# A gated mix of segmented attention and a GLU: the first segment of x comes in transposed, and two weights change queues

## The chip, the cores and the metric

The kernel runs on one core of one Trainium2 chip. The core has TensorE (PE), VectorE (DVE), ScalarE (ACT), GpSimd (POOL) and SyncE (SP); transfers are issued by SP and ACT and carried by 16 DMA engines. The metric is the device time of one execution in microseconds (us), lower is better.

## The reference

The input x has 2048 tokens of 512 features. Two branches read it, and a gate for each token mixes them:

```python
q, k, v = x @ wq, x @ wk, x @ wv              # 32 heads of 16, 4 segments of 512 tokens
for s in range(4):                             # A: attention with a memory
    a_dot = softmax(q_s @ k_s.T / 4, causal) @ v_s
    a_mem = (phi(q_s) @ M) / (phi(q_s) @ z + 1e-6)
    o_s = sigmoid(beta) * a_mem + (1 - sigmoid(beta)) * a_dot
    M, z = M + phi(k_s).T @ v_s, z + phi(k_s).sum()
a = o @ wo
b = (gelu(x @ w_gate) * (x @ w_up)) @ w_down   # B: GLU, 512 -> 1792 -> 512
g = sigmoid((x * gate_w).sum(-1))
out = g * a + (1 - g) * b
```

`phi(t)` is `t + 1` for positive t and `exp(t)` otherwise. All tensors are bf16.

## The kernel before

The kernel makes one pass over four segments of 512 tokens, `s = 0..3`. Everything that multiplies x needs it with features on the partitions: the tile `xT[s % 3]` holds four blocks `kb` of 128 features by 512 tokens. From it `project` computes for four blocks `t` of 128 columns the keys `K{s}_{t}` and queries `Q{s}_{t}` (each 4 matmuls of 512 columns into one PSUM bank, then an eviction `Kev`, `Qev`), and the values `V{s}_{m}a` and `V{s}_{m}b` for four blocks of 128 tokens. The keys are copied twice with masks into `kD` (`kpada`, `kpadb`). `glu_gate` and `glu_up` compute 14 blocks each of the GLU (`G`, `U`), `outputs` the products with `w_down` (`out`) and `wo` (`wo`), the mix (`oev`) and the store (`dma`).

Attention works in fills. A fill `st{s}_{t}{A..E}` writes scores of four head groups into all four banks of `XALL` (psX), one exponential `exp` on ACT takes all 2048 columns out, POOL masks the diagonal blocks (`msk`), and after eight key blocks `pv{s}_{t}` multiplies by the values. As there is one `XALL`, a fill waits for the exponential before it. For the memory, `phk` is computed on DVE and ACT, turned by transposing transfers (`ktr`), and multiplied with the values (`mz`); reading it takes `phq`, `nd`, `ndp` and transposing transfers of the result (`otr`).

Nothing is scheduled at run time. All work is named tasks; the string `ORDER` lists them, and each engine gets its own tasks in the order of that list. `name:d` or `name:a` says whether DVE or ACT does an eviction, `name:3` gives a PSUM bank. Waits are derived from what a task reads and writes. An engine and a DMA queue work strictly in that order, so a task that waits holds back all that follows on its engine.

The start is what the change touches. The first segment's x comes in with tokens on the partitions, in three plain transfers `x0_0` (128 KB, SP), `x0_1` (128 KB, ACT) and `x0_2` (256 KB, SP) into the tile `pt[5]`, used later for probabilities. `xtr0_{h}{p}` turns it on TensorE with an identity matrix into `XALL`, four turns each for half `h` of the tokens and pair `p` of feature blocks, and `xev0_{h}{p}` copies the turned blocks to `xT[0]`. The first keys are summed in three parts: `K0_{t}a` (blocks 2 and 3, first 256 tokens), `K0_{t}b` (blocks 0 and 1, the same tokens), `K0_{t}c` (all blocks, last 256 tokens). The key weights come as two halves, `wk1` (blocks 2 and 3) on SP and `wk0` on ACT. SP then issues `wq0` after `wk1` has landed, the gate row `gw`, `wq1` after `wk0`, `wv` after `x0_2`, `beta`, the four transposing transfers of segment 1 (`x1_0` to `x1_3`, after `wq0`), and the GLU weights in halves `wg0`, `wu1`, `wg1`, `wu0`. Six matmuls on zeros (`warm1`) run on TensorE while the first data come. Segments 1 to 3 always came by transposing transfers (line 344).

The list of early waits, as the code has it, with the names of the loads waited for at the end:

```python
ld_w("wq0", SP, wq[:, halves[0], :], wsrc(A_wq)[:, halves[0], :], [("wq", 0)], 0.25, ["wk1"])
ld_w("wq1", SP, wq[:, halves[1], :], wsrc(A_wq)[:, halves[1], :], [("wq", 1)], 0.25, ["wk0"])
ld_w("wv", SP, wv[:, :, 0:512], wsrc(A_wv), [("wv",)], 0.5, ["x0_2"])
ld_xt(1, "wq0")
```

Of the kernel before, what the change touches and what calls it, by code (L numbers as in the profile page):

```python
# [246 lines left out]
def _build(es, nc, A_x, A_wq, A_wk, A_wv, A_wo, A_beta, B_w_gate, B_w_up, B_w_down, gate_w, out):  # L247
# [216 lines left out]
    def xk(s, i):  # L464
        return [("xT", s % R_XT, i), *([("xT", 0, i, "h0")] if s == 0 else [])]

    def project(s):
        b, b3 = s % 2, s % R_XT
        k0 = [Slot() for _ in range(4)]
        for nm, kbs, h in (("a", (2, 3), 0), ("b", (0, 1), 0), ("c", (0, 1, 2, 3), 1)) if s == 0 else ():  # L470
            for t in range(4):
                one(f"K0_{t}{nm}", PE, len(kbs) * T_MM / 2, [I(lambda e, t=t, i=i, h=h: e.matmul(
                    BK[k0[t].i][:, 256 * h:256 * h + 256], wk[:, i, t * 128:(t + 1) * 128], xT[0][:, i, 256 * h:256 * h + 256],
                    start=(i == 2 - 2 * h), stop=(i == 1 + 2 * h)), [("xT", 0, i, "h0"), ("wk", i),
                    *([("xT", 0, i)] if h else [])], [bk(k0[t])]) for i in kbs], opens=(nm == "a"))
# [291 lines left out]
    XB = XALL.bitcast(BF)  # L767
    for h in range(2):
        for p in (1, 0):
            j = 2 * h + p  # L770
            one(f"xtr0_{h}{p}", PE, 4 * T_TR, [I(lambda e, q=q, kb=kb, j=j: e.transpose(
                XB[:, 1024 * j + (kb % 2) * 256 + (q % 2) * 128:1024 * j + (kb % 2) * 256 + (q % 2) * 128 + 128],
                pt[stage[0]][:, q, kb * 128:(kb + 1) * 128], ident[:, :]),
                [("xs", 0, 2 * h), ("xs", 0, 2 * h + 1), ("pt", stage[0]), ("ident",)], [("X", j)]) for kb in (2 * p, 2 * p + 1) for q in (2 * h, 2 * h + 1)])
            dst = xT[0][:, 2 * p:2 * p + 2, 256 * h:256 * h + 256]
            xin = XB[:, 1024 * j:1024 * j + 512].rearrange("p (k c) -> p k c", c=256)
            wr = [("xT", 0, kb, "h0") if h == 0 else ("xT", 0, kb) for kb in (2 * p, 2 * p + 1)]
            task(f"xev0_{h}{p}", [
                (ACT, 0.477, [I(lambda e, dst=dst, xin=xin: e.activation(dst, xin, ACTF.Copy), [("X", j)], wr)]),
                (DVE, 0.335, [I(lambda e, dst=dst, xin=xin: e.tensor_copy(dst, xin), [("X", j)], wr)])], L_DVE)  # L780

# [66 lines left out]
ld_x0_0 warm0 warm1:0 ld_x0_1 ident xtr0_01 ld_wk0 masks vones0 causal1 causal0 gwz ld_wk1 ld_x0_2 ld_wq0 xev0_01:d  # L848
ld_gw consts xtr0_00 K0_1a:1 K0_2a:2 K0_3a:3 K0_0a:0 ld_wq1 ld_wv ld_beta xtr0_10 xtr0_11 xev0_00:a K0_2b K0_3b K0_1b
K0_0b xev0_11:a xev0_10:d K0_0c Kev0_0:d kpadb0_0 kpada0_0 K0_3c Kev0_3:a K0_1c K0_2c Kev0_2:d Kev0_1:d kpada0_1  # L850
Q0_0:0 Q0_3:3 Qev0_0:a st0_0A exp0_0A ld_x1_1 ld_x1_0 ld_x1_2 ld_x1_3 gwtr:2 gwev Qev0_3:d phka0_0 Q0_1:1 V0_3b:0
V0_0b:2 V0_2a:3 Vev0_3b:d st0_0B Vev0_0b:d ld_wg0 V0_1a:0 V0_3a:2 phkb0_0 Vev0_2a:d Qev0_1:d Vev0_1a:d Vev0_3a:d
V0_2b:3 Q0_2:1 V0_0a:0 exp0_0B st0_0C exp0_0C V0_1b:2 Vev0_2b:d betab Qev0_2:d Vev0_1b:a bexp Q1_1:3 Q1_2:1 kpadb0_1
Vev0_0a:d causal msk0_0A phkc0_0 vsh0_00 vsh0_01 vsh0_20 Qev1_2:d st0_0D V1_2b:0 G0_1:2 G0_3:1 exp0_0D st0_0E
Vev1_2b:d kpada0_3 exp0_0E V1_3a:0 Vev1_3a:a kpada0_2 Gev0_1:d Gev0_3:d Qev1_1:d G0_5:2 G0_0:1 st0_1A G1_3:3 V1_1b:0
msk0_0B Gev0_5:d vsh0_21 Gev0_0:d Gev1_3:d msk0_0D gqa msk0_0C kpadb0_2 Vev1_1b:d msk0_0E pv0_0:21 exp0_1A st0_1B
gfull tp0_d00 kpadb0_3 V1_0a:3 G0_4:0 msk0_1A G1_0:2 Vev1_0a:d phka0_2 tp0_d01 Gev0_4:d exp0_1B st0_1C exp0_1C msk0_1B
msk0_1C phkb0_2 Q1_0:3 G0_2:1 V1_3b:0 gqb pvp0_00 Qev1_0:d Gev1_0:d Vev1_3b:d Gev0_2:d phkc0_2 ld_wu1 ld_wg1 ld_wu0
ktr0_1 ld_x2_0 st0_1D exp0_1D G1_2:3 K1_0:2 K1_3:0 Gev1_2:d Kev1_3:d st0_2A G0_6:1 V1_2a:3 Vev1_2a:d Gev0_6:d Kev1_0:a
gz0 msk0_1D pv0_1:20 exp0_2A st0_2B exp0_2B ktr0_2 tp0_d10 pvp0_01 tp0_d11 pvp0_10 K1_1:3 Q1_3:1 Qev1_3:d Kev1_1:d  # L860
kpadb1_3 gelu0 G0_7:2 G1_1:0 Gev1_1:d gd0_7 st0_2C G1_4:1 G0_13:3 ktr0_0 Gev1_4:d phka1_0 ld_x2_2 ld_x2_3 G0_9:0
G0_10:1 G0_12:2 gd0_9 gd0_10 gd0_13 gd0_12 G0_8:0 ld_x2_1 vsh1_21 phqa1_0 pvp0_11 vsh1_20 ld_wd1 G0_11:1 K1_2:3
kpadb1_1 ota0_0 Kev1_2:d gd0_8 gd0_11 U0_10:2 V1_0b:0 h0_10 exp0_2C U0_7:1 Q2_1:3 V1_1a:2 ktr0_3 phka1_2 kpada1_3
Vev1_0b:d h0_7 kpada1_2 Qev2_1:d Vev1_1a:a st0_2D exp0_2D U0_11:0 U0_2:1 h0_11 h0_2 phqa1_2 mz0:2 phkb1_0 mza0 phkc1_0
st0_2E U0_4:3 K2_0:0 U0_13:1 h0_4 h0_13 kpada1_0 kpadb1_0 Kev2_0:d exp0_2E st0_3A exp0_3A msk0_2A msk0_2B msk0_2C
msk0_2D msk0_2E U0_9:2 pv0_2:31 st0_3B phkb1_2 exp0_3B h0_9 tp0_d21 G1_5:0 U0_5:2 U0_8:1 Gev1_5:a gr0 phkc1_2 tp0_d20
st0_3C h0_8 K2_3:3 Kev2_3:d U0_3:0 h0_3 pvp0_21 kpada1_1 U0_6:1 h0_5 h0_6 exp0_3C phqb1_2 st0_3D Q2_0:3 Q2_3:0 U0_1:2
exp0_3D Qev2_3:a Qev2_0:d h0_1 pvp0_20 kpadb2_3 st1_0A V2_2b:1 U0_0:3 exp1_0A phqb1_0 h0_0 msk0_3A msk0_3B msk0_3C gz1
goa0 gob0 msk0_3D pv0_3:02 st1_0B exp1_0B tp0_d31 tp0_d30 K2_2:3 U0_12:2 Vev2_2b:d kpadb1_2 Kev2_2:d V2_0b:0 V2_2a:1
st1_0C Vev2_0b:a exp1_0C Vev2_2a:d kpada2_2 h0_12 kpada2_3 phqc1_2 G1_6:3 K2_1:0 Kev2_1:d V2_1b:1 msk1_0B st1_0D  # L870
exp1_0D ld_wd0 kpadb2_1 ktr1_1 vsh1_00 Gev1_6:a out0_1_0:2 out0_0_0:0 st1_0E out0_0_1 out0_1_1 V2_0a:3 exp1_0E
Vev2_1b:d mzq0 Vev2_0a:d out0_0_2 out0_1_2 msk1_0C msk1_0E msk1_0A msk1_0D goc0 G1_8:1 G1_7:3 kpada2_0 ota0_2 wev0_1:d
# [73 lines left out]
```

## Time and profile before

| what | value |
|---|---|
| median of 3 runs | 265.31 us (265.06 to 265.48) |
| the profiled execution | 265.46 us |
| its span, first to last instruction | 263.7 us |
| HBM read and written | 8.14 MB and 2.10 MB |
| x transposed, issue on SP to landing | 2.4 to 4.3 us |

The page of the profile gives for each engine its busy time, then the span in 40 slices, then the chain of work that ended last: followed back from the last instruction, at each step to what released it. A line such as `9.92 1.47 PE psD L446 x6` in that chain is a start, a length, an engine, a tile, a line of the code and a count of instructions. In the timeline the form is the same, with the operation and shapes added, and in square brackets the idle time of the engine and what ended it. SPq and ACTq are the issue of transfers by SP and ACT. In the sums by stretch the columns are the window in us, its length, the busy time and number of instructions of PE, PEld (weight loads), DVE, ACT and POOL, then the granted clock, the mean share of the DMA engines and GB/s. Some matmul records can be missing from a trace.

### The profile page before, as it was taken

The page shows a single profiled execution, that of the slowest core. Times are in us where ns is not written, and L with a number is a line of the kernel's source. Part 1 is how long each engine was busy: PE and PEld are TensorE (multiplying, and loading weights), DVE is VectorE, ACT ScalarE, POOL GpSimd, SP SyncE. Part 2 cuts the span into 40 slices and gives each one's busy share as a digit, 9 for nine tenths or more (in the row PEclk, how much of TensorE's full clock was granted, in tenths as well). Part 3 has the DMA queues.
Part 4 walks back from the last instruction along what each step waited for, and adds up shares of the span by engine and source line. Part 5 has one row for each costly group of instructions (what it writes and reads, how often), then busy time and mean ns, then how long its engine had stood idle before and what let it go on. Part 6 is the DMA issues. An engine that isn't in the chain of part 4 may idle for free.

```text
span 263.7 us, 6622 instructions
## 1 busy us (share of the span) xinstructions
PE 254.3 (96%) x2775; PEld 120.4 (46%) x2815; DVE 207.9 (79%) x427; ACT 197.7 (75%) x159; POOL 99.8 (38%) x164
## 2 busy tenths in 40 slices
...
PEclk9999999999999999999999999999999999999999
...
DMA packets 31302, 16.50 MB, mean 63 GB/s; under 512 B 20776, under 2 KB 31272, under 8 KB 31272
## 3 DMA queue, kind: packets, MB, share of 16 engines
...
HBM read 8.14 MB, written 2.10 MB: 39 GB/s over the span
## 4 chain that ended last, share of the span: by engine, by line
PE 91%; DVE 3%; DMA 3%; issue 2%; SPq 0%
PE psD L446 45%; PE psD L718 17%; PE psX L598 8%; PE psD L640 7%; PE psD L495 6%; PE psD L732 5%; DMA wq<-in_A_wq_dram 2%; DMA wk<-in_A_wk_dram 1%; PE psD L543 1%; DVE omem L557 1%; DVE ost L736 1%; DVE tT L526 0%; PE psD L573 0%; SPq L340 0%; DVE rcm L556 0%
## 5 line engine op out<-in xcount | busy, mean ns | idle before, releaser
L604 ACT ACTIVATE pt<-psX 128x2048 bf16<-128x2048 f32 x72 | 135.1, 1876 | 41.2 <-PE psX L598 41.0
L610 POOL TENSOR_TENSOR pt<-pt,ctri 128x256 bf16<-128x256 bf16 x128 | 92.2, 726 | 145.3 <-ACT pt L604 117.4
L446 PE MATMUL psD<-xT,wu 128*128 128x512 bf16 x213 | 52.4, 379 | 1.3 <-issue 0.9
L718 PE MATMUL psD<-wd,gb 128*128 128x512 bf16 x213 | 51.8, 379 | 1.2 <-issue 1.0
L446 PE MATMUL psD<-xT,wg 128*128 128x512 bf16 x214 | 51.3, 379 | 1.0 <-issue 0.5
L703 DVE TENSOR_TENSOR gb<-psD,gb 128x512 bf16<-128x512 f32 x56 | 37.4, 680 | 4.9 <-PE psD L446 4.7
L446 PEld LDWEIGHTS psD<-xT,wg 128*128 128x128 bf16 x224 | 20.7, 98 | 24.9 <-issue 1.9
L526 DVE STREAM_TRANSPOSE tT<-psD 128x512 f32<-128x512 f32 x32 | 22.3, 705 | 12.3 <-PE psD L640 12.2
L446 PEld LDWEIGHTS psD<-xT,wu 128*128 128x128 bf16 x224 | 20.6, 98 | 24.1 <-issue 1.7
L718 PEld LDWEIGHTS psD<-wd,gb 128*128 128x128 bf16 x224 | 20.3, 98 | 23.9 <-issue 2.8
L598 PE MATMUL psX<-qT,kD 32*128 32x192 bf16 (+7 forms) x512 | 28.5, 287 | 0.0
L640 PE MATMUL psD<-pt,vnat 64*17 64x128 bf16 (+7 forms) x512 | 18.7, 283 | 0.0
L651 DVE SCALAR_TENSOR_TENSOR ob<-tT,gq,rc 128x256 bf16<-128x256 f32 x32 | 17.8, 556 | 1.1
L495 PE MATMUL psD<-wv,xT 128*128 128x256 bf16 (+1 forms) x128 | 18.5, 273 | 0.0
L640 PE MATMUL psD<-pt,vsh 64*17 64x128 bf16 (+7 forms) x512 | 18.3, 283 | 0.0
L598 PEld LDWEIGHTS psX<-qT,kD 32*128 32x128 bf16 x512 | 8.2, 92 | 21.3 <-ACT pt L604 8.9
L440 DVE CAST gb<-psD 128x512 bf16<-128x512 f32 x24 | 16.0, 681 | 2.4 <-PE psD L446 2.4
L686 ACT ACTIVATE gb<-psD 128x512 bf16<-128x512 f32 x28 | 15.4, 594 | 3.1 <-PE psD L446 2.8
L736 DVE SCALAR_TENSOR_TENSOR ost<-psD,gtok,wds 128x512 bf16<-128x512 f32 (+2 forms) x18 | 12.2, 686 | 6.1 <-PE psD L732 5.3
L440 DVE CAST kT<-psD 128x512 bf16<-128x512 f32 x14 | 9.5, 687 | 8.5 <-PE psD L446 7.3
L446 PE MATMUL psD<-xT,wq 128*128 128x512 bf16 x61 | 15.5, 380 | 0.5 <-DMA wq<-in_A_wq_dram 0.2
L732 PE MATMUL psD<-wo,oT 128*128 128x512 bf16 (+2 forms) x71 | 15.8, 356 | 0.0
...
## 6 DMA issues: line engine op xcount, KB each, us to landing
...
wq<-in_A_wq_dram SPq DMA_DIRECT2D x2, 256.0 KB, 3.3
...
```

The costliest lines, as they stand in the source:

```text
L440: (DVE, 0.60, [I(lambda e: e.tensor_copy(dst, src()), [bk(sl), *reads], writes)]),
L446: one(name, PE, n * T_MM, [I(lambda e, i=i: e.matmul(BK[sl.i][:, :], lhs(i), rhs(i), start=(i == 0), stop=(i == n - 1)), reads(i), [bk(sl) ...
L495: one(f"V{s}_{m}{'ab'[hf]}", PE, 2 * T_MM, [I(lambda e, i=i, sl=sl, a=a, z=z, xs=xs: e.matmul(BK[sl.i][:, 0:z - a], xs(i), wv[:, i, a:z], ...
L526: one(f"tp{name}", DVE, 0.605, [I(lambda e, sl=sl, ti=ti: e.transpose(tT[ti][:, :], BK[sl.i][:, :]), [bk(sl)], [("tT", ti)])], bias=bias)
L598: ins.append(I(lambda e, t=t, kb=kb, ncol=ncol, c0=c0, g=g: e.matmul(XALL[:, g * 512 + c0:g * 512 + c0 + ncol], kD[b][32 * g:32 * g + 32, ...
L604: one(f"exp{s}_{name}", ACT, 2048 * 0.000833 + 0.05, [I(lambda e: e.activation(pt[slot][:, :, :], xin, ACTF.Exp, scale=ATT_SCALE), [("X",) ...
L610: ins.append(I(lambda e, mv=mv: e.tensor_tensor(mv, mv, cm, ALU.mult), [("pt", slot), ("causal",)], [("pt", slot)]))
L640: ins.append(I(lambda e, kb=kb, slot=slot, c0=c0, n=n, g=g, r0=r0, sl=banks[j], va=va: e.matmul(BK[sl.i][32 * g:32 * g + 17, 64 * kb:512], ...
L651: I(lambda e, ti=ti, ri=ri, t=t, j=j, dst=dst: e.scalar_tensor_tensor(out=dst, in0=t_rows(ti), scalar=gq[:, 2 * t + j:2 * t + j + 1], in1= ...
L703: one(f"h{s}_{ft}", DVE, 0.605, [I(lambda e, sl=sl, gi=gi, f=f: e.tensor_tensor(gb[gi][:, f, :], BK[sl.i][:, :], gb[gi][:, f, :], ALU.mult ...
L718: mm.append(I(lambda e, fb=fb, gi=gi, f=f, q=q, sl=sl: e.matmul(BK[sl.i][:, :], gb[gi][:, f, q], wd[:, fb, :], start=(fb == 0), stop=(fb = ...
L732: one(f"wo{s}_{qt}{sfx}", PE, 4 * T_MM * w / 512, [I(lambda e, kb=kb, q=q, so=so, c=c, w=w: e.matmul(BK[so.i][:, 0:w], oT[:, kb, q], wo[:, ...
```

## The change

The first segment's x is loaded like the other segments', by four transposing transfers on SP, one for each block of 128 features, blocks 3, 2, 1, 0 in this order. The turns `xtr0`, their evictions `xev0` and the plain loads of x are gone. All four early halves of `wk` and `wq` are issued by ACT: `wk1`, `wk0`, and, after `wk0` has landed, `wq1` and `wq0`. `wv` on SP waits for `x0_1`, now the transposed block 1, and segment 1's x for `wq1`. The first keys are summed one feature block at a time into `XALL` (one bank for each `t`) over all 512 tokens, and evicted from there; the first queries are two tasks each, `Q0_{t}1` (blocks 3 and 2) and `Q0_{t}0`. `ORDER` is written anew throughout; apart from these tasks it names the same ones.

```diff
-    stage = (R_PT - 1, R_PT - 2)
...
+    def ld_x0(kb):
+        load(f"x0_{kb}", SP, lambda e: e.dma_start_transpose(xT[0][:, kb, :], A_x[0, 0:512, kb * 128:(kb + 1) * 128]),
+             [("xT", 0, kb)], issue=1.31, lat=3.0)
...
-    xin0 = A_x[0, 0:512, :].rearrange("(q p) d -> p q d", p=P)
-    for eng, nm, q in ((SP, "0", slice(0, 1)), (ACT, "1", slice(1, 2))):
-        ld_w(f"x0_{nm}", eng, pt[stage[0]][:, q, :], xin0[:, q, :], [("xs", 0, q.start)], 0.125)
-    for eng, h in ((SP, 1), (ACT, 0)):
-        ld_w(f"wk{h}", eng, wk[:, halves[h], :], wsrc(A_wk)[:, halves[h], :], [("wk", 2 * h), ("wk", 2 * h + 1)], 0.25)
-    ld_w("x0_2", SP, pt[stage[0]][:, halves[1], :], xin0[:, halves[1], :], [("xs", 0, 2), ("xs", 0, 3)], 0.25)
+    for kb in (3, 2, 1, 0):
+        ld_x0(kb)
+        if kb >= 2:
+            h = kb - 2
+            ld_w(f"wk{h}", ACT, wk[:, halves[h], :], wsrc(A_wk)[:, halves[h], :], [("wk", 2 * h), ("wk", 2 * h + 1)], 0.25)
     ld_w("gw", SP, gw4, gate_w.rearrange("(kb p) -> kb p", p=P), [("gw4",), ("gwz",)], 0.01)
-    ld_w("wq0", SP, wq[:, halves[0], :], wsrc(A_wq)[:, halves[0], :], [("wq", 0)], 0.25, ["wk1"])
-    ld_w("wq1", SP, wq[:, halves[1], :], wsrc(A_wq)[:, halves[1], :], [("wq", 1)], 0.25, ["wk0"])
-    ld_w("wv", SP, wv[:, :, 0:512], wsrc(A_wv), [("wv",)], 0.5, ["x0_2"])
+    ld_w("wq1", ACT, wq[:, halves[1], :], wsrc(A_wq)[:, halves[1], :], [("wq", 1)], 0.25, ["wk0"])
+    ld_w("wq0", ACT, wq[:, halves[0], :], wsrc(A_wq)[:, halves[0], :], [("wq", 0)], 0.25, ["wk0"])
+    ld_w("wv", SP, wv[:, :, 0:512], wsrc(A_wv), [("wv",)], 0.5, ["x0_1"])
...
-    ld_xt(1, "wq0")
+    ld_xt(1, "wq1")
...
+        for kb in (3, 2, 1, 0) if s == 0 else ():
             for t in range(4):
+                one(f"K0_{t}{kb}", PE, T_MM, [I(lambda e, t=t, kb=kb: e.matmul(
+                    XALL[:, 512 * t:512 * t + 512], wk[:, kb, t * 128:(t + 1) * 128], xT[0][:, kb, :],
+                    start=(kb == 3), stop=(kb == 0)), [("xT", 0, kb), ("wk", kb)], [("X", t)])])
+        for h in (1, 0) if s == 0 else ():
+            for t in range(4):
+                one(f"Q0_{t}{h}", PE, 2 * T_MM, [I(lambda e, t=t, kb=kb: e.matmul(
+                    BK[q0[t].i][:, :], wq[:, kb, t * 128:(t + 1) * 128], xT[0][:, kb, :],
+                    start=(kb == 3), stop=(kb == 0)), [("xT", 0, kb), ("wq", h)], [bk(q0[t])])
+                    for kb in (2 * h + 1, 2 * h)], opens=(h == 1))
```

The first lines of the new order, with the start of TensorE's stream, and its last line:

```
ld_x0_3 ld_x0_2 ld_wk1 ld_x0_1 ld_x0_0 warm0 warm1:0 K0_33 K0_32 consts ld_wk0 ident gwz vones0 K0_03 K0_13 causal0
K0_02 K0_23 causal1 K0_12 masks K0_22 ld_wq1 ld_wq0 ld_gw ld_wv K0_01 K0_11 K0_31 K0_21 K0_00 K0_10 Kev0_1:a Q0_01:1
K0_30 Q0_00 K0_20 Kev0_0:d kpada0_0 kpadb0_0 Kev0_3:a Q0_31:2 gwtr:3 Q0_30 Qev0_0:a Kev0_2:d st0_0A exp0_0A kpadb0_2
gwev Q0_11:0 ld_x1_1 ld_x1_0 ld_x1_2 ld_x1_3 ld_beta V0_1b:1 Vev0_1b:d Qev0_3:d Q0_10 V0_2a:3 V0_1a:1 Qev0_1:d phka0_0
...
wo3_3c:1 wev3_3:a dma13 dma12 oev3_3c oev3_3a wo3_2:2 dma15c oev3_2 dma15a dma14 wo3_3b:3 oev3_3b dma15b
```

SP's transfers between segment 1's x and segment 2's memory read, in the new order: `beta`, `wg0`, one `vsh`, `wu1`, three `vsh`, `x2_1`, `ktr0_1`, `ktr0_0`, `wg1`, `x2_3`, `ktr0_3`, `wu0`, `x2_2`, `x2_0`, `wd1`, `ktr0_2`. Before they were: `wg0`, four `vsh`, `wu1`, `wg1`, `wu0`, `ktr0_1`, `x2_0`, `ktr0_2`, `ktr0_0`, `x2_2`, `x2_3`, `x2_1`, two `vsh`, `wd1`, `ktr0_3`. (`vsh` are copies of value rows for the second head of a pair; `ktr0` are the turns of `phk` of segment 0.)

More of the change, by code (lines that the diff above doesn't have):

```diff
@@ L464, in xk @@
     def xk(s, i):
-        return [("xT", s % R_XT, i), *([("xT", 0, i, "h0")] if s == 0 else [])]
+        return [("xT", s % R_XT, i)]
     def project(s):
         b, b3 = s % 2, s % R_XT
-        k0 = [Slot() for _ in range(4)]
-        for nm, kbs, h in (("a", (2, 3), 0), ("b", (0, 1), 0), ("c", (0, 1, 2, 3), 1)) if s == 0 else ():
+        q0 = [Slot() for _ in range(4)]
+        for kb in (3, 2, 1, 0) if s == 0 else ():
             for t in range(4):
[L472 to L475, printed above, removed]
@@ new lines, in project @@
+        for h in (1, 0) if s == 0 else ():
[4 more added lines that the diff above has]
+                    for kb in (2 * h + 1, 2 * h)], opens=(h == 1))
+        for t in range(4):
+            if s == 0:
+                xin = XALL[:, 512 * t:512 * t + 512]
+                task(f"Kev0_{t}", [
+                    (ACT, 0.477, [I(lambda e, t=t, xin=xin: e.activation(kT[:, t, :], xin, ACTF.Copy), [("X", t)], [("kT", 0, t)])]),
+                    (DVE, 0.60, [I(lambda e, t=t, xin=xin: e.tensor_copy(kT[:, t, :], xin), [("X", t)], [("kT", 0, t)])])], L_DVE)
+            else:
+                sl = dense(f"K{s}_{t}", lambda i, t=t: wk[:, i, t * 128:(t + 1) * 128], lambda i: xT[b3][:, i, :],
+                           lambda i: [*xk(s, i), ("wk", i)], 4)
+                evict(f"Kev{s}_{t}", kT[:, t, :], sl, [], [("kT", 0, t)])
@@ L485, in project @@
                       [("kT", 0, t), (mk.name,)], [("kD", b, t, nm)])])
-            sl = dense(f"Q{s}_{t}", lambda i, t=t: wq[:, i, t * 128:(t + 1) * 128], lambda i: xT[b3][:, i, :],
+            sl = q0[t] if s == 0 else dense(f"Q{s}_{t}", lambda i, t=t: wq[:, i, t * 128:(t + 1) * 128], lambda i: xT[b3][:, i, :],
                        lambda i: [*xk(s, i), ("wq", i // 2)], 4)
@@ L765, in head_gates @@
             I(lambda e: e.tensor_scalar(gfull[:], gfull[:], 1.0, None, ALU.add), [("gfull",)], [("gfull",)])], bias=-150.0)
[L767 to L780, printed above, removed]
     head_gates()
@@ L847 @@
 ORDER = """
[L848 to L872, printed above, removed]
@@ new lines @@
+Gev0_1:d Gev1_0:d G0_0:2 exp0_0E bexp st0_1A exp0_1A Gev0_0:d Vev1_0b:d kpada0_2 msk0_0B ld_wu1 vsh0_00 vsh0_20
+vsh0_21 msk0_0D msk0_0A msk0_0C msk0_0E G1_3:0 V1_2b:1 G0_3:2 Vev1_2b:d kpada0_3 Gev0_3:d Gev1_3:d phkb0_0 st0_1B
+pv0_0:31 exp0_1B tp0_d01 phkc0_0 tp0_d00 G0_4:2 V1_1b:0 st0_1C Gev0_4:a V1_3b:1 G0_2:2 Q1_0:3 exp0_1C st0_1D msk0_1A
+msk0_1B Vev1_3b:d Vev1_1b:d ld_x2_1 gqa Qev1_0:d Gev0_2:d G1_2:1 K1_0:0 K1_3:3 phkb0_2 phkc0_2 Gev1_2:d Kev1_3:d
+exp0_1D st0_2A exp0_2A ktr0_1 ktr0_0 msk0_1C gqb msk0_1D G0_6:2 pv0_1:13 Kev1_0:d Gev0_6:d st0_2B exp0_2B ld_wg1
@@ new lines @@
+ld_x2_3 ktr0_3 ld_wu0 ld_x2_2 ld_x2_0 tp0_d10 ld_wd1 ktr0_2 G1_4:0 pvp0_00 kpadb1_3 Q1_3:2 K1_1:1 Gev1_4:d tp0_d11
+Qev1_3:d pvp0_11 G0_10:0 G1_1:3 Gev1_1:d Kev1_1:d G0_8:2 st0_2C G0_9:3 gelu0 gd0_10 gd0_9 G0_7:1 gd0_7 gd0_8 G0_12:0
+gd0_12 G0_11:3 G0_13:1 V1_2a:2 gd0_11 gd0_13 exp0_2C U0_7:0 K1_2:3 pvp0_10 kpada1_0 phka1_0 h0_7 phqa1_2 kpadb1_0
+Kev1_2:d kpada1_3 Vev1_2a:d Q2_1:1 U0_10:0 h0_10 phkb1_0 mz0:3 mza0 phqa1_0 phkc1_0 st0_2D U0_2:2 U0_11:0 exp0_2D
+U0_13:3 st0_2E h0_11 U0_9:0 kpada1_1 h0_2 h0_13 gz1 msk0_2B msk0_2A msk0_2C msk0_2D gz0 U0_4:2 V1_3a:3 h0_9 phka1_2
@@ new lines @@
+gob0 phqc1_2 pvp0_21 kpadb1_2 h0_12 ld_wo Gev1_5:d Kev2_2:d pvp0_31 vsh1_00 vsh1_01 out0_1_0:3 out0_1_1 exp1_0C st1_0D
+exp1_0D V2_2b:2 V2_1a:1 out0_1_2 Vev2_1a:a Vev2_2b:a V2_0a:0 msk1_0C goa1 st1_0E exp1_0E goc0 pvp0_30 Vev2_0a:d
+V2_1b:1 Vev2_1b:d phqc1_0 kpadb2_0 V2_3b:2 Vev2_3b:d wev0_1:d V2_0b:0 out0_0_0:1 out0_0_1 out0_0_2 ota0_2 wev0_0:d
+phka2_0 Vev2_0b:d ota0_3 G1_8:2 G1_7:3 gelu1 gd1_8 msk1_0D msk1_0A G1_13:1 G1_11:0 gd1_7 gd1_11 G1_9:2 gd1_9 gd1_13
+msk1_0B gfull msk1_0E G1_10:3 gd1_10 G1_12:0 gd1_12 wo0_1:2 st1_1A nd1_0:1 V2_3a:3 V2_2a:0 oev0_1 U1_9:2 ndp1_0
```

99 lines of the change are left out of this document (48 added, 51 removed).

## The prediction

> **What bounds the kernel now.** I read the engine totals first, then the chain of waits, then the instructions of the first 12 us in order of time, then the sums by stretch, the DMA landings and the tail.
>
> ```profile
> span 263.7 us, 6622 instructions
> ...
> PE 254.3 (96%) x2775; PEld 120.4 (46%) x2815; DVE 207.9 (79%) x427; ACT 197.7 (75%) x159; POOL 99.8 (38%) x164
> ...
> PEclk9999999999999999999999999999999999999999
> ...
> PE 91%; DVE 3%; DMA 3%; issue 2%; SPq 0%
> ...
> wq<-in_A_wq_dram SPq DMA_DIRECT2D x2, 256.0 KB, 3.3
> ...
> xT<-in_A_x_dram SPq DMA_TRANSPOSE x12, 3.5
> ```
>
> TensorE is nearly always busy, and the chain lies on it for 91%. The gaps of 0.16 to 0.22 us that the waits call "issue" are no loss: there are 2815 weight loads and 2775 matmuls, so 40 matmul records are missing, and each such gap is as long as one matmul of 512 columns (24 of them take 5.18 us in the chain, 0.216 each). TensorE therefore waits for nothing from 9.92 us to its last matmul, and the chain's start says what set 9.92:
>
> ```profile
> 1.25 3.76 DMA wk<-in_A_wk_dram
> ...
> 5.03 0.37 SPq L340
> ...
> 5.89 3.98 DMA wq<-in_A_wq_dram
> ...
> 9.92 1.47 PE psD L446 x6
> ```
>
> SP first had to see wk1 land (5.01), then issued wq0, the gate row and wq1, and wq1 landed 3.98 us after its issue. All before 9.92 was ended by DMA; the timeline shows what TensorE did meanwhile:
>
> ```profile
> 1.04 2.74 PE L380 MATMUL psD<-warm 128*128 128x512 bf16 x6 [1.04 <-POOL warm L376]
> ...
> 3.83 0.81 PE L771 MATMUL psX<-ident,pt 128*128 128x128 bf16 x8
> ...
> 5.14 1.03 PE L472 MATMUL psD<-xT,wk 128*128 128x256 bf16 x8 [0.50 <-DMA wk<-in_A_wk_dram]
> ...
> 6.02 0.62 PE L771 MATMUL psX<-ident,pt 128*128 128x128 bf16 x8
> ...
> 6.48 2.78 PE L472 MATMUL psD<-xT,wk 128*128 128x256 bf16 x24
> ...
> 7.66 5.12 SPq L344 DMA_TRANSPOSE xT<-in_A_x_dram x4
> ...
> 9.31 0.38 PE L446 MATMUL psD<-xT,wq 128*128 128x512 bf16 x1
> ```
>
> **What is removed.** The 16 turns (0.81 and 0.62 us) and their four evictions (0.42 us twice on DVE, 0.60 twice on ACT) all lie before 9.92, in time that the query weights hold anyway: 0 by themselves. The first keys keep their columns: 32 matmuls of 256 were 16 of 512, 3.45 us either way, also under the same wait.
>
> **The break-even.** At 9.92 all keys and 2 of the 16 first query matmuls were done (six of the first eight remain, 6 x 0.216 = 1.29, and the fill starts at 11.32), so 14 were left. The new order reaches its last early load, wq0, at Q0_00, with those 14 and one key matmul (K0_20) left: 15. Both streams then are the same length if Q0_00 starts at 9.92 - 0.22 = **9.70**. Each 0.1 us earlier is 0.1 us won, as long as the rest stays dense.
>
> **When the rows of x land.** Four transposes go first on SP; four of the same took 5.12 us to issue, 1.28 each, so the issues start at 0.79, 2.07, 3.35 and 4.63. Landing took 2.4 to 4.3 us over the twelve. I take 2.9, the shortest of segment 1's four, since nothing stands ahead of these in SP's queue: the last row at 7.5 (7.0 to 8.9). Before Q0_00 stand five matmuls on it (K0_00, K0_10, two of Q0_01, K0_30), 1.08 us: Q0_00 not before 8.6 (8.1 to 10.0).
>
> **When the weights land.** ACT now issues wk1, wk0, waits for wk0, then wq1, wq0. As the second issue on ACT wk0 landed 4.1 us after 1.21, at 5.3, with 1 MB in flight; after the change 1 MB is again in flight by then (wk and x), so 5.3, with 0.3 either way. An ACT issue takes 0.41 to 0.47, so wq0 goes out at 5.75. The two wq loads took 2.6 and 4.0 (the page's median is 3.3): wq0 lands at 5.75 + 3.3 = **9.05** (8.35 to 9.75, and 8.05 to 10.05 with wk0's 0.3). This is later than 8.6, so weights still set the start: 9.05 - 9.70 = **-0.65**.
>
> Two views speak on the second queue. In the stretches one queue moved 178 to 188 GB/s around wq, two together 379:
>
> ```profile
> 4.00:5.00 1.00, 0.64 (x8) 0.47 (x6) 0.42 (x1) 0.32 (x1) 0.93 (x4) 1.00 1.08 379
> ...
> 7.00:8.00 1.00, 1.00 (x11) 0.90 (x10) 0.01 (x1) 0.28 (x1) 0.00 (x0) 1.00 0.73 178
> ...
> 9.00:10.00 1.00, 0.72 (x5) 0.27 (x4) 1.00 (x4) 0.02 (x1) 0.00 (x0) 1.00 1.01 354
> ```
>
> But the third stretch has 354 on SP alone, so I count nothing for rate. The Trainium skill's page "DMA: Bandwidth & Descriptors" (Issuing engines are not separate DMA queues) says that all queues run on the same 16 engines and a second issuer saves only issue time; the 354 agrees with it, the 178 does not by itself. By that rule nothing is won through ACT's queue but the place in line, and the sum stays as it is. By the 379 of the first stretch wq0 would land near the low end, 8.35: the first rival.
>
> **What the moved issues delay.** On ACT the table load (1.28 us, at 1.72 before) now stands behind wq0's issue, 6.2 to 7.5; the first eviction there is K0_10's at 8.1: 0, and 0.6 if wk0 were that late. On SP wv waits for row 1 (3.35 + 2.9 = 6.3) and the issue at 6.4 with 5.0 to land gives 11.4; its first user comes 2.5 us after Q0_00 (eleven matmuls and the fill), 11.55: 0, but with only 0.15 to spare. x of segment 1 waits for wq1 (about 8.2), takes 5.12 to issue, and lands by 16.3; its first user stands 7.6 us after Q0_00, at 16.7: 0. wg0 follows beta at 13.8 and lands 5 to 6 us on, 19 to 20, against a user at 20.2: 0. wg1 stands behind two key turns on SP, which wait for DVE's phi: issue near 33 instead of 23.05, landing 39.4 (up to 40.5 with 7.5 as before), user at about 40.5: 0, and a microsecond if DVE's phi is a microsecond late; wu0, the x of segment 2 and wd1 queue behind wg1, with 4 us and more to their users.
>
> **The rest of the order.** Work and instruction kinds are the same. A fill costs 0.10 before and 0.11 after it, a PV block 0.10; the order puts a fill behind a PV block 14 times in both texts, so this is 0, with 0.3 either way for the few pairs that differ. Whether a dependency now ends late somewhere cannot be read from before, whose order has none: at least 0, at most about half an exponential (1.88 us, the longest step that a fill waits for), 0.9. I take 0, nearest to the row I have. **The tail** changes the last piece: the query tile's 512-column mix (0.75 us on DVE, then a 128 KB store, 1.8) gave the end; now a 128-column one (0.35, store 1.5) follows it. Mix start 0.22 earlier against the PE's end, plus 0.35, plus 1.5 against 1.8: 0, 0.2 either way.
>
> **Sum.** -0.65 and zeros. The profiled execution took 265.46 around its span of 263.7; the median of the runs is 265.31, so 265.31 - 0.65 = 264.66.
>
> **Rivals.** (1) Rows and weights both quick: wq0 at 8.35, rows at 8.1, start 8.35: -1.35, **263.96**. For it speaks the 379 GB/s, against it that transposes share the engines. (2) A wait replaced by its like: wq0 takes the 4.0 of before's second wq load, lands at 9.75: +0.05, **265.4**. For it: wv now runs beside it. (3) The other side: **the clock**. The six warm-up matmuls took 0.457 us each, those from 5.14 on 0.13 per 256 columns or less, so full speed came between 3.8 and 5.1, while the turns ran (the page's clock line reads 9 from its first slice on and cannot show it; the durations do). They are gone; from 3.78 TensorE now has one matmul (row 3) until row 2 at 2.07 + 2.9 = 5.0. If the clock stays low until as much work has passed as at first (4.1 us, from 1.04 to 5.14), it rises at 9.1: nine matmuls fit at 0.457, and the nine still ahead of Q0_00, less the one at the boundary, take 8 x 0.216, so Q0_00 starts at 10.8: +1.1, **266.4**. It decides once Q0_00 would be ready after 9.70. Against it: the warm-up itself is untouched. The Trainium skill's page "TensorE: Matmul & The Clock Gate" (Part 1) has a free-running window of about 3.4 us that the work must fill, and Part 4 says that turns do not count as work there; by the first the removed turns could cost a window, by the second nothing, and by the second alone the sum stays at 264.66. (4) The SP line: wg1 late by 1 us at its user, or a like stall from the new order, with the start as forecast: +0.35 to +0.9, up to **266.2**.
>
> **Chances.** Forecast 0.42, (1) 0.12, (2) 0.18, (3) 0.15, (4) 0.13. About 0.2% (0.53 us) is what a measurement tells from no change. The forecast lies close to this bound: 0.28 of its 0.42 below 264.78, the rest within. Faster 0.28 + 0.12 = 0.40; same 0.14 and 0.14 of (2), 0.28; slower 0.04 of (2), (3) and (4), 0.32. The likeliest case's own range is 264.2 to 265.2; to hold eight in ten the range runs from (1) to nearly (3), 264.0 to 266.3.
>
> **What would show it.** Right: Q0_00 near 9.05, ended by a wq DMA, with row 0 landed before 7.9; key matmuls at 0.216; the chain dense on PE until the end. Wrong: wq0 landing after 9.7; matmuls at 0.43 past 5 us; a wait for wg, wv or a DVE step in the chain after 10 us; a landing of x above 3.5.

## The result, and the profile after

| kernel | median us | lowest to highest | runs |
|---|---|---|---|
| before | 265.31 | 265.00 to 265.85 | 13 |
| after | 267.11 | 266.21 to 268.46 | 13 |

The change made the kernel slower: the ratio is 1.0072, with an interval of 1.0055 to 1.0090. The forecast was 264.7, so even its range (to 266.3) did not hold the time. The profiled execution after took 266.49 around a span of 264.8, 1.1 more than before; the median rose by 1.8. The single times after spread over 2.2 us, those before over 0.9, so the profiled execution is one of the shorter ones of its kernel.

The page after, in the lines that were shown of before (span; busy time of the engines; the chain of waits by engine; the early transfers), reads:

```profile
span 264.8 us, 6592 instructions
...
PE 258.0 (97%) x2783; PEld 118.2 (45%) x2783; DVE 205.8 (78%) x423; ACT 198.3 (75%) x159; POOL 95.8 (36%) x164
...
PE 95%; DMA 2%; SPq 1%; DVE 0%; issue 0%; DVEq 0%
...
wq<-in_A_wq_dram ACTq DMA_DIRECT2D x2, 256.0 KB, 4.1
```

This trace has as many matmul as weight-load records, so the "issue" gaps of before are gone from the chain without any time having been won. The kernel is bound as before; the question is where the start went. TensorE's timeline, and the end of the chain of waits ahead of it (start, length, what):

```profile
1.05 2.74 PE L377 MATMUL psD<-warm 128*128 128x512 bf16 x6 [1.05 <-POOL warm L373]
5.49 2.93 PE L469 MATMUL psX<-xT,wk 128*128 128x512 bf16 x12 [1.70 <-DMA xT<-in_A_x_dram]
9.30 0.60 PE L469 MATMUL psX<-xT,wk 128*128 128x512 bf16 x2 [0.88 <-DMA xT<-in_A_x_dram]
9.74 0.59 PE L474 MATMUL psD<-xT,wq 128*128 128x512 bf16 x2
10.18 0.38 PE L469 MATMUL psX<-xT,wk 128*128 128x512 bf16 x1
10.39 0.59 PE L474 MATMUL psD<-xT,wq 128*128 128x512 bf16 x2
```

```profile
4.64 0.04 issue
4.68 4.57 DMA xT<-in_A_x_dram
9.26 0.05 issue
9.30 0.60 PE psX L469 x2
```

TensorE stands idle twice, both times for x: 1.70 us for row 3, 0.88 for row 0. Row 0, issued at 4.68, took 4.57 to land; `wq0`, issued at 5.52, landed at 9.83. Q0_00 (the second L474 line) starts at 10.39, 0.69 behind the break-even of 9.70. Row 3 alone had put the forecast start of 9.05 out of reach: it landed at 5.45, 4.65 us after its issue, and 17 matmuls of 0.216 (8 of rows 3 and 2, 4 of row 1, 5 in line behind row 0) stand ahead of Q0_00, so the earliest start was 5.49 + 3.67 = 9.16. The sums by stretch show the transfers meanwhile (window, its length, busy time of PE, PEld, DVE, ACT, POOL, then clock, DMA share, GB/s):

```profile
5.00:6.00 1.00, 0.51 (x2) 0.21 (x3) 0.00 (x0) 0.00 (x0) 0.04 (x1) 1.00 0.49 108
6.00:7.00 1.00, 1.00 (x6) 0.42 (x5) 0.00 (x0) 0.89 (x1) 0.00 (x0) 1.00 0.98 115
7.00:8.00 1.00, 1.00 (x6) 0.45 (x5) 0.00 (x0) 0.40 (x1) 0.00 (x0) 1.00 0.79 176
8.00:9.00 1.00, 0.42 (x2) 0.00 (x0) 0.00 (x0) 0.00 (x0) 0.00 (x0) 1.00 1.11 302
```

From 6 to 8 us the DMA engines are 79 to 98% busy and move 115 to 176 GB/s: there the small packets of the rows (256 bytes) and the first packets of `wq` (1,024 bytes, from ACT's queue) run together. The first ten packets of `wq`, between 6.5 and 7.0, took 687 ns each in the mean; from 7.5 on, by half microseconds, such a packet took 50 to 69.

### The profile page after: what moved, and what is told of

It is laid out like the page before. It is cut to its first block, busy times and chain, and to the rows that moved or that the text cites. A ratio compares the mean times of both kernels' runs of the same rounds, so it can differ in the third digit from the quotient of the medians.

```text
span 264.8 us, 6592 instructions
## 1 busy us (share of the span) xinstructions
PE 258.0 (97%) x2783; PEld 118.2 (45%) x2783; DVE 205.8 (78%) x423; ACT 198.3 (75%) x159; POOL 95.8 (36%) x164
## 4 chain that ended last, share of the span: by engine, by line
PE 95%; DMA 2%; SPq 1%; DVE 0%; issue 0%; DVEq 0%
PE psD L443 46%; PE psD L726 19%; PE psX L606 9%; PE psD L648 7%; PE psD L503 5%; PE psD L740 5%; DMA xT<-in_A_x_dram 2%; PE psD L551 1%; SPq L348 1%; PE psD L474 1%; PE psD L581 1%; PE psX L469 0%; DVE ost L744 0%; DVEq L796 0%; PE psD L760 0%
## 5 line engine op out<-in xcount | busy, mean ns | idle before, releaser
L612 ACT ACTIVATE pt<-psX 128x2048 bf16<-128x2048 f32 x72 | 135.1, 1877 | 40.1 <-PE psX L606 39.4
L618 POOL TENSOR_TENSOR pt<-pt,ctri 128x256 bf16<-128x256 bf16 x128 | 89.0, 702 | 152.6 <-ACT pt L612 134.7
L443 PE MATMUL psD<-xT,wu 128*128 128x512 bf16 x224 | 54.6, 380 | 0.0
L443 PE MATMUL psD<-xT,wg 128*128 128x512 bf16 x224 | 53.2, 380 | 0.0
L726 PE MATMUL psD<-wd,gb 128*128 128x512 bf16 x224 | 53.1, 380 | 0.0
L659 DVE SCALAR_TENSOR_TENSOR ob<-tT,gq,rc 128x256 bf16<-128x256 f32 x32 | 19.3, 602 | 1.1
L648 PE MATMUL psD<-pt,vnat 64*17 64x192 bf16 (+7 forms) x512 | 18.9, 283 | 0.0
L648 PE MATMUL psD<-pt,vsh 64*17 64x64 bf16 (+7 forms) x512 | 18.3, 283 | 0.0
L503 PE MATMUL psD<-wv,xT 128*128 128x257 bf16 (+1 forms) x128 | 18.0, 273 | 0.0
L503 PEld LDWEIGHTS psD<-wv,xT 128*128 128x128 bf16 x128 | 12.0, 97 | 6.3 <-DVE vnat L510 0.2
L648 PEld LDWEIGHTS psD<-pt,vnat 64*17 64x17 bf16 x512 | 11.4, 86 | 7.2 <-issue 3.4
```

The lines of the kernel that those rows point to most:

```text
L443: one(name, PE, n * T_MM, [I(lambda e, i=i: e.matmul(BK[sl.i][:, :], lhs(i), rhs(i), start=(i == 0), stop=(i == n - 1)), reads(i), [bk(sl) ...
L503: one(f"V{s}_{m}{'ab'[hf]}", PE, 2 * T_MM, [I(lambda e, i=i, sl=sl, a=a, z=z, xs=xs: e.matmul(BK[sl.i][:, 0:z - a], xs(i), wv[:, i, a:z], ...
L612: one(f"exp{s}_{name}", ACT, 2048 * 0.000833 + 0.05, [I(lambda e: e.activation(pt[slot][:, :, :], xin, ACTF.Exp, scale=ATT_SCALE), [("X",) ...
L618: ins.append(I(lambda e, mv=mv: e.tensor_tensor(mv, mv, cm, ALU.mult), [("pt", slot), ("causal",)], [("pt", slot)]))
L648: ins.append(I(lambda e, kb=kb, slot=slot, c0=c0, n=n, g=g, r0=r0, sl=banks[j], va=va: e.matmul(BK[sl.i][32 * g:32 * g + 17, 64 * kb:512], ...
L659: I(lambda e, ti=ti, ri=ri, t=t, j=j, dst=dst: e.scalar_tensor_tensor(out=dst, in0=t_rows(ti), scalar=gq[:, 2 * t + j:2 * t + j + 1], in1= ...
```

## The experiments

All medians in us; "before" is the kernel before, run on the same chip between them. The first four kernels ran on one chip, the next four on a second, e_best and e_best2 on a third, e_best3 and b_fill on a fourth; the kernel before differs between these chips by up to 0.3 in the median, so times of different groups are compared by their distance to it. The ratio is not formed from the medians: a few long executions of the kernel before (up to 267.7) count in it, so it is mostly lower than theirs (not for e_best2).

| kernel | median | lowest to highest (runs) | before | ratio, interval |
|---|---|---|---|---|
| a_again | 267.15 | 266.00 to 267.78 (10) | 265.70 | 1.0039, 1.0014 to 1.0065 |
| e_nowait | 270.16 | 269.62 to 270.83 (4) | 265.70 | 1.0150, 1.0102 to 1.0198 |
| e_wqsp | 267.46 | 266.27 to 268.51 (10) | 265.70 | 1.0051, 1.0024 to 1.0078 |
| e_touch | 267.56 | 266.45 to 268.91 (10) | 265.70 | 1.0058, 1.0029 to 1.0087 |
| e_warm | 266.21 | 265.98 to 266.86 (12) | 265.55 | 1.0015, 0.9996 to 1.0034 |
| e_cold | 268.16 | 267.55 to 268.36 (6) | 265.55 | 1.0081, 1.0052 to 1.0109 |
| e_oldord | 267.09 | 265.70 to 268.08 (12) | 265.55 | 1.0051, 1.0030 to 1.0072 |
| e_oldord_warm | 265.81 | 265.40 to 266.55 (12) | 265.55 | 1.0003, 0.9988 to 1.0018 |
| e_best | 266.34 | 266.04 to 266.69 (6) | 265.55 | 1.0024, 1.0007 to 1.0041 |
| e_best2 | 266.20 | 265.78 to 267.01 (12) | 265.55 | 1.0029, 1.0019 to 1.0039 |
| e_best3 | 266.24 | 265.91 to 266.73 (12) | 265.37 | 1.0030, 1.0013 to 1.0047 |
| b_fill | 265.65 | 265.11 to 268.15 (12) | 265.37 | 1.0010, 0.9988 to 1.0032 |

**Why row 0 lands late.** First the kernel after once more, unchanged, beside the others.

> The changed kernel once more, for a second trace. Theory (start): its span is that of the kernel before (263.7 us) plus the start of Q0_00 less 9.70, plus 0.4 that is not placed yet; if the landing of row 0 of x differs from 9.25 us, the span moves with it one for one. Rival (the rest of the order): the span moves by waits after 13 us while row 0 lands at about 9.25 again.

Row 0 landed at 8.85 instead of 9.25, Q0_00 started at 9.98 instead of 10.39, and the span was 264.4 instead of 264.8: the end follows the start one for one in this pair, as the break-even has it.

Then `wq` without its wait, issued by ACT at 1.78 and 2.30:

```diff
-    ld_w("wq1", ACT, ..., [("wq", 1)], 0.25, ["wk0"])
-    ld_w("wq0", ACT, ..., [("wq", 0)], 0.25, ["wk0"])
+    ld_w("wq1", ACT, ..., [("wq", 1)], 0.25)
+    ld_w("wq0", ACT, ..., [("wq", 0)], 0.25)
```

> wq1 and wq0 are issued by ACT right behind wk0, with no wait for its landing. Theory (the first packets of wq, 350 to 770 ns each, hold back row 0 of x): those packets now come before 5 us, row 0 lands at 7.6 to 8.2 instead of 9.25, Q0_00 starts at about 8.9, the time falls by 1.2 to 1.6 us against the changed kernel, to about 265.6. Rival (two queues merely share the engines; the bytes are the same): row 0 still lands after 8.8 and the time moves by less than 0.4 us.

It was 4.5 us slower than before. `wq0` did land earlier, at 8.67, but rows 2, 1 and 0 came at 8.88, 9.10 and 9.48. In the chain of waits, and in TensorE's timeline:

```profile
2.09 6.79 DMA xT<-in_A_x_dram
8.93 4.89 PE psX L469 x13
```

```profile
8.93 4.67 PE L469 MATMUL psX<-xT,wk 128*128 128x512 bf16 x12 [2.21 <-DMA xT<-in_A_x_dram]
```

Row 2 took 6.79 us from its issue, though it stood second in SP's own queue: 0.75 MB of plain transfers were issued on ACT's queue ahead of it, and 0.25 MB more 0.2 us behind it. The 12 matmuls behind it take 4.67 us where they took 2.93, a low clock as well. Here my expectation fell outright.

The counter-test puts `wq` behind the rows on SP:

```diff
-    ld_w("wq1", ACT, ..., ["wk0"])
-    ld_w("wq0", ACT, ..., ["wk0"])
+    ld_w("wq1", SP, ..., ["wk0"])
+    ld_w("wq0", SP, ..., ["wk0"])
```

> wq1 and wq0 are issued by SP behind the four rows of x, the rest as in the changed kernel. Theory (first packets of wq): they start 0.9 us later and in SP's own line, behind row 0, which lands at 7.5 to 7.9; wq0 then lands near 10 and sets the start, so the time is within 0.5 us of the changed kernel, but the chain's early piece is wq and not x. Rival (row 0 is slow by itself): row 0 lands at about 9.2 with wq out of its way.

```profile
5.71 3.24 PE L469 MATMUL psX<-xT,wk 128*128 128x512 bf16 x14 [1.92 <-DMA xT<-in_A_x_dram]
9.45 0.60 PE L474 MATMUL psD<-xT,wq 128*128 128x512 bf16 x2 [0.49 <-DMA wq<-in_A_wq_dram]
```

With no plain transfer beside it row 0 landed at 7.33, 2.66 us after its issue, and 14 matmuls run without a gap. But now `wq` is late: `wq1` lands at 9.40, `wq0` at 10.11, Q0_00 starts at 10.16, and the time is that of the kernel after. So row 0's delay goes with `wq` beside it, and here, whichever of the two went first, the other was late. Two things stay open. In six of the seven traces that have all four weight halves as in after, `wk0` before `wq` on ACT's queue with the wait between, row 0 took 4.13 to 4.93 us, but in e_warm (below) 2.86, although `wq` was issued at 5.56 and 5.96; the other six issue `wq1` at 5.04 to 5.49. And the row's packets tell only half of the delay: the last of them ended at 7.82 in after and at 6.89 in e_wqsp, so that 1.43 us pass from there to the landing in the one and 0.45 in the other. What holds the landing back that long is not shown.

Last, whether the slow first packets of `wq` come from touching that memory for the first time: 64 bytes of each of its rows are read early, on ACT.

```diff
+    tch = sb("tch", [P, 4, 32])
+    ld_w("tch", ACT, tch[:], wsrc(A_wq)[:, :, 0:32], [("tch",)], 0.03)
```

> One small transfer more: ACT reads 64 bytes of every row of wq into an unused tile, ahead of wq1 and wq0 and behind wk0 without a wait. Theory (a first touch of the tensor in HBM costs the slow packets): the slow packets move to the small transfer, wq's own packets stay near 50 ns from the first on, row 0 lands before 8.3 and the time falls by 0.6 to 1.2 us. Rival (any burst of two queues is slow): row 0 lands at about 9.2 again and the time is the same or later.

Row 0 landed at 8.81, and the 37 packets of `wq` between 6.5 and 7.0 took 118 ns each in the mean. In a_again, without the touch, 20 packets took 181 in the same half microsecond. This settles nothing on the first packets. What it did show is a start of the first score product at 13.11, 1.1 us later than in after although row 0 came earlier: the key matmuls stand 0.43 us apart until 9.7. That led to the clock.

**The clock.** The first pair changes one number, the count of warm-up matmuls, to 12 and to 1:

```diff
-    ... [("warm",)], [bk(s0)]) for _ in range(6)], ...
+    ... [("warm",)], [bk(s0)]) for _ in range(12)], ...
```

> The kernel after, with 12 warm-up matmuls instead of 6, so that TensorE has work from the start until about row 3's landing (6 took until 3.78 us; 6 more at 0.22 to 0.43 each reach 5.1 to 6.4). Clock theory (in about half of the runs of the kernel after, TensorE's idle time from 3.78 to 5.5 us makes the granted clock rise one window later, about 1.5 us lost): the long runs vanish, median 266.1 to 266.6, all runs within 0.8 us, no row 0 later than before. Rival (the scatter comes from the transfers of the start, whose landings differ from run to run): median 267.1 as for the kernel after, scatter 1.5 to 2 us as before.

> The kernel after, with 1 warm-up matmul instead of 6: TensorE has next to no work until row 3 lands at about 5.5 us. Clock theory: the clock rises late in every run, the first key matmuls stand 0.43 us apart until about 9.7 us or later, first score product at 13 us or later, median 268 to 269. Rival (the clock is not decided by this work): median 267.1, K0 matmuls 0.22 apart from 6 us on in the profiled run.

Twelve warm-ups take the median from 267.11 to 266.21 and the spread from 2.2 to 0.9 us; one warm-up gives 268.16. As the times come from different chips, the distance to the kernel before is the better measure: it falls from 1.80 and 1.45 (after and a_again) to 0.66, by 0.8 to 1.1 us. Both came out as the clock theory said (the spread a little above the 0.8 expected), although the twelve kept TensorE until 6.15, 0.2 us past row 3's landing (5.92). In e_warm row 0 landed at 7.53 and TensorE never waited for it, yet Q0_00 started only at 10.05: the 17 matmuls ahead of it, the first still 0.42 us apart, fill the time from 6.15 on. The two timelines:

```profile
1.05 5.30 PE L377 MATMUL psD<-warm 128*128 128x512 bf16 x12 [1.05 <-POOL warm L373]
6.15 3.42 PE L469 MATMUL psX<-xT,wk 128*128 128x512 bf16 x14
```

```profile
1.05 0.61 PE L377 MATMUL psD<-warm 128*128 128x512 bf16 x1 [1.05 <-POOL warm L373]
5.89 5.89 PE L469 MATMUL psX<-xT,wk 128*128 128x512 bf16 x14 [4.23 <-DMA xT<-in_A_x_dram]
```

The same 14 key matmuls take 3.42 us in the one and 5.89 in the other, and 3.24 in e_wqsp with six warm-ups and an early clock.

**The order.** Then the start of the kernel after, up to the first score product, with the order of before from there; once with 6 and once with 12 warm-ups. The whole text behind `exp0_0A` is exchanged, with the banks of the four Q0 tasks renamed to fit:

```diff
-... Q0_01:1 K0_30 Q0_00 ... Q0_31:2 gwtr:3 Q0_30 ... st0_0A exp0_0A kpadb0_2 gwev Q0_11:0 ...
+... Q0_01:0 K0_30 Q0_00 ... Q0_31:3 Q0_30 ... st0_0A exp0_0A ... gwtr:2 gwev ... Q0_11:1 Q0_10 ...
```

> The start of the kernel after (its loads, K0 and the two halves of Q0, up to the first score product), and from there the order of the kernel before. Order theory (0.4 us were lost spread over the new order, behind the start): from the start of Q0_00 to the last matmul 250.7 us instead of 251.1, so with Q0_00 at 10.0 to 10.4 a profiled run of 265.6 to 266.1 and a median of 266.6 to 266.9 (the late clock untouched). Rival (the 0.4 belong to the start's own new parts, such as the split Q0, or to the instruction stream as a whole): 251.1 us again, median 267.1.

> Both: the start of the kernel after with 12 warm-up matmuls, and the order of the kernel before from the first score product on. Theory of three terms (late start of Q0_00 0.3 to 0.7, order 0.4, late clock 0.6 to 0.9 in the median): only the late start is left, median 265.6 to 266.1, that is 0.3 to 0.7 above the kernel before on the same chip. Rival (one of the two terms is not what it is taken for): 266.5 or more.

With 12 warm-ups 0.40 us is won against e_warm (265.81 against 266.21), as expected. With six, the median is 267.09 against 267.11 for the kernel after, and nothing is seen of the 0.4: the expected 266.6 to 266.9 fell. A late clock in most of these runs would explain it: the twelve times go from 265.70 to 268.08 and seven are above 267, but only the profiled execution, at 267.39, shows its clock. On this chip and with this order the six further warm-ups are worth 267.09 - 265.81 = 1.28. The timeline of the profiled execution, and the stretches around the rise:

```profile
5.69 5.47 PE L469 MATMUL psX<-xT,wk 128*128 128x512 bf16 x14 [1.90 <-DMA xT<-in_A_x_dram]
11.00 0.59 PE L474 MATMUL psD<-xT,wq 128*128 128x512 bf16 x2
```

```profile
8.00:9.00 1.00, 1.00 (x4) 0.30 (x2) 0.00 (x0) 0.00 (x0) 0.00 (x0) 1.00 1.15 289
9.00:10.00 1.00, 1.00 (x4) 0.38 (x3) 0.00 (x0) 0.00 (x0) 0.00 (x0) 1.00 0.97 316
10.00:11.00 1.00, 1.00 (x6) 0.38 (x5) 0.02 (x1) 0.00 (x0) 0.00 (x0) 1.00 1.25 255
```

TensorE is busy throughout, but four matmuls start in each microsecond until 10 and six after it. The clock column says 1.00 in all three, and so does the page's clock line: only the spacing of the matmuls shows it. (The trace's own record of the clock begins with the rise, here at 10.33, and the views count the time before it as full speed; the traces of after and a_again hold no record at all.) Row 0 had landed at 8.85 and `wq0` at 9.40, so in this execution neither counts; without the late clock Q0_00 could have started as in e_oldord_warm, at 9.99, and it started at 11.64.

From the start of Q0_00 to the end of the span it is 254.4 us in after, a_again, e_wqsp and e_warm, and 254.0 in e_oldord_warm and in e_oldord; before, from the break-even, it was 263.7 - 9.70 = 254.0. So the new order costs 0.3 to 0.4 wherever the start lies, with six warm-ups too. Two thirds of it are on TensorE: from Q0_00 to the end of TensorE's last piece in the chain 251.12 in e_warm against 250.90 in e_oldord_warm. One wait of the size is seen, in the timeline of after; e_warm has it too, e_oldord_warm has not:

```profile
104.51 1.24 PE L726 MATMUL psD<-wd,gb 128*128 128x512 bf16 x5
...
105.79 0.11 PEld L551 LDWEIGHTS psD<-mzq,phq 128*128 128x128 bf16 x2 [0.53 <-DVE omem L565]
105.79 0.29 PE L551 MATMUL psD<-mzq,phq 128*128 128x136 bf16 x2
```

Five matmuls of the product with `w_down`, 0.216 each, end at 105.59 if they start at 104.51; the product with the memory (`nd1_5`) has to wait until DVE has read its bank, 0.2 us. The rest is the tail, from there to the end of the span: 3.27 us in e_warm, 3.16 in e_oldord_warm.

**A start built from this.** Three tries to have rows, weights and matmuls out of each other's way, with the old order behind them. All keep SP's four transposes. In e_best `wq1` takes `wk0`'s place at the front, and TensorE works off what has landed:

```diff
+    ld_w("wk1", ACT, ...)
+    ld_w("wq1", ACT, ...)
+    ld_w("wk0", ACT, ..., ["wq1"])
+    ld_w("wq0", ACT, ..., ["wq1"])
...
+K0_33 K0_03 K0_13 K0_23 K0_32 K0_02 K0_12 K0_22 Q0_01:0 Q0_31:3 Q0_11:1 K0_01 ... Q0_00 ... Q0_30 Q0_10 st0_0A
```

e_best2 leaves only `wk1` at the front (`wq1` and `wk0` wait for it) and has 8 warm-ups; e_best3 is e_best with all of K0 ahead of Q0's rest and `gwtr gwev` ahead of the first score product.

> A start built from what the runs showed, with 12 warm-up matmuls and from the first score product on the order of the kernel before: the second weight transfer at the front of ACT's queue is wq1 instead of wk0, the matmuls go by what has landed (K0 of rows 3 and 2, six matmuls of Q0 of these rows, then K0 of rows 1 and 0, then the rest of Q0), and wk0 and wq0 are issued when wq1 has landed. Theory (TensorE lost 0.45 us waiting for row 0 in the kernel with old order and 12 warm-ups; here it has 14 matmuls, 3.0 us, before it needs rows 1 and 0 or wk0, that is until about 8.9): wk0 lands at 8.7 to 9.2, no or little wait, median 265.2 to 265.6, 0.2 to 0.6 below that kernel's 265.81 and even with or just below the kernel before. Rival (wk0 or row 0 land later than 9.3, as wq0 did, and TensorE waits as long as before): 265.8 or more.

> The same, but only wk1 at the front of ACT's queue, with wq1 and wk0 issued when wk1 has landed (3.8 us) and 8 warm-up matmuls. Theory (plain transfers of ACT's queue hold the transposes back): with less in front of them rows 3 and 2 land 0.5 to 1 us earlier, at 4.6 to 5.6, wq1 at about 7.1 and wk0 at 7.5 to 8, rows 1 and 0 later, at 7.5 to 9; K0 starts at about 5, with a wait of up to 0.7 for wq1: median 264.9 to 265.6. Rival (the rows come no earlier, they are held by the issue of SP alone): K0 at 5.5 or later and a wait for wq1, 265.6 to 266.5.

> The kernel e_best with its two new waits mended: all of K0 ahead of Q0's rest, so that the key evictions and masks are done when the first score product comes, and the gate column's turn and copy ahead of it. Theory (e_best lost 0.26 us before the first score product and 0.54 before V0 to the order of these few instructions): 0.6 to 0.8 less than e_best, median 265.5 to 265.8, no wait over 0.3 us after 9 us. Rival (wv's landing, not the gate column, set V0's wait): the 0.4 to 0.5 stay, 266.0 or more.

The transfers came nearly as expected (in e_best `wk0` at 8.9; in e_best2 row 3 at 4.58, but `wq1` only at 7.76) and the start was nearly dense, yet all three are 0.6 to 0.9 slower than before and none of the three expected medians came. In e_best2 the clock rose only at 6.67, so that its first key matmuls, from 4.63 on, stand 0.43 us apart. In e_best TensorE then waits 0.36 us for the gate column ahead of V0; in e_best3, where that is mended, it waits for ACT at the second score product:

```profile
12.67 0.40 PE L605 MATMUL psX<-qT,kD 32*128 32x512 bf16 x4
13.00 1.49 PE L502 MATMUL psD<-wv,xT 128*128 128x257 bf16 x12
15.04 0.40 PE L605 MATMUL psX<-qT,kD 32*128 32x448 bf16 x8 [0.56 <-ACT pt L611]
```

In e_oldord_warm four query matmuls behind the first score product (from 11.96 on) cover this exponential; moved ahead to fill the wait for the rows, they are missing there. No version beat the kernel before; e_oldord_warm comes level with it.

**The long executions of before.** Six short matmuls fill TensorE's idle time behind its first turns (4.4 to 5.1 us):

```diff
+    one("warm2", PE, 0.4, [I(lambda e: e.matmul(BK[s1.i][:, 0:P], warm[:, :], warm[:, :], ...)) for _ in range(6)], ...)
```

> The kernel before, with six short matmuls (128 columns each) behind the turns of the first rows, where TensorE stood idle from 4.4 to 5.1 us in its profile. Clock theory (the kernel before has the late clock too, in the few of its runs that are 1.3 to 2.5 us above its median): none of its runs is over 266.5, the median stays at 265.4 to 265.7. Rival (these runs have another cause): some runs at 267 and above, as in the kernel before. With so few such runs a result without any is weak evidence.

One run of 12 took 268.15, so the theory is not borne out, and what makes some executions of the kernel before long (8 of the 54 beside the kernels from a_again to e_oldord_warm were above 266.2) stays open. The profiled execution, one of the short ones, shows how much of a late clock this start hides: by the trace's record its clock rose at 6.06, in the kernel before's at 4.30; its last 24 key matmuls start at 6.91 instead of 6.48, but the first score product starts at 11.36 against 11.32.

## Why the prediction was wrong

**Right.** The bound; the break-even of 9.70 (e_oldord_warm starts Q0_00 at 9.99 and has a span of 264.0, 0.3 above 263.7); `wk0`'s landing (5.3 forecast, 5.09); the moved transfers on SP, of which none was waited for (`wg1` landed at 39.3, forecast 39.4). Of these, the landing of `wg1` is partly luck: it was issued at 34.2 instead of 33 and took 5.1 us instead of 6.4. That the turns and evictions were worth nothing by themselves was not tested.

**Wrong, the row landing.** The step that failed is "I take 2.9, the shortest of segment 1's four, since nothing stands ahead of these in SP's queue". Nothing did, but `wq` on ACT's queue ran beside it: 4.57 and 4.17 us in the kernel after, 2.66 in e_wqsp without it. The profile of before already had the difference: segment 1's rows took 4.26, 4.03, 3.43 and 2.88 us in the order of their issue, and the last, issued at 11.52, was the only one issued after `wv` had landed (11.34). Row 3 was late in the same way, 4.65 instead of 2.9 with `wk` beside it, and the prediction counted only the 5 matmuls behind row 0, not the 17 behind row 3. The landing of 8.85 to 9.25 lies at or beyond the bound of 8.9. `wq0`, taken as 3.3 after its issue, took 4.31 and 3.9 in the two traces. Each was costed as if the other were not there, and the -0.65 became +0.28 (Q0_00 at 9.98) to +0.69 (10.39).

**Wrong, the order.** "Work and instruction kinds are the same" held, and the counts of switches did too; but a dependency that ends late, costed at 0 out of a range up to 0.9, is there (0.2), and the tail cost 0.1, inside its "0, 0.2 either way". Together 0.3 in the traces, 0.4 in the medians.

**Wrong, the weight of the third rival.** The clock got a chance of 0.15 and 1.1 us. It is the largest term: 0.8 to 1.3 in the median, and up to 1.65 in the Q0_00 of a single one (11.64 against 9.99). The rival let TensorE idle from 3.78 to row 2 at 5.0 with one matmul between; it idled until row 3 at 5.5 to 5.9. The doubt against it, that the warm-up itself is untouched, weighed the wrong thing: with more work after the sixth warm-up the long runs went. That the turns had been this work is not shown: in the profiled execution of before the clock rose at 4.30, while they ran, and in e_wqsp, without them, at 4.38. The Trainium skill's page "TensorE: Matmul & The Clock Gate" (Part 1) says that the rise depends on a free-running window of about 3.4 us; the runs agree: after the work began for good, the spacing shrank 3.9 us later in e_nowait and e_touch, 4.6 in e_oldord and 5.5 in e_cold, between one and two such windows. In e_wqsp it rose 3.3 us after the first warm-up and 0.6 us after the last had ended, so there it did not take a whole window of work.

**The sum as it was.** On the chip of e_warm to e_oldord_warm: late start 265.81 - 265.55 = 0.26, order 266.21 - 265.81 = 0.40, clock 267.09 - 265.81 = 1.28, together 1.94. With the clock taken from the kernel after, 267.11 - 266.21 = 0.90 across two chips, it is 1.56. The change itself measured 1.80 in the result and 1.45 (267.15 - 265.70) with a_again, so the sum closes only as well as the clock's term is known. The 0.26 by itself lies within the interval of its ratio (0.9988 to 1.0018) and rests on the trace, 9.99 against 9.70.

**Rivals 1, 2 and 4.** The first did not come: a second queue gave no rate for both. The second was right on `wq0` (9.75 forecast, 9.83 and 9.39) but row 0 came on top. Of the fourth, the new order's stall is real at 0.2 and the SP line is not.
